# A graph network's edge step on one core: overlapping stages of units, small groups first, and pairs of chunks in one adding scatter

## The chip, the cores and the metric

The kernel runs on one core of one Trainium2 chip. The metric is the time of one execution on the device in microseconds (us). Of the version before there are three runs: 10865.60, 10892.54 and 10880.72 us, median 10880.72 us.

## The reference

12500 nodes have 64 features each; 800000 edges, in random order, name a source and a destination node and have 16 features of their own. Each edge makes a message, messages are summed by destination, and the nodes are updated:

```python
def reference(x, e_attr, src, dst, w_msg, w_upd):
    N, D = x.shape                      # 12500, 64; e_attr is [800000, 16]
    m_in = jnp.concatenate([x[src], x[dst], e_attr], axis=-1)
    msg = _silu(m_in @ w_msg)           # [800000, 64]
    agg = _segment_sum(msg, dst, N)
    return _silu(jnp.concatenate([x, agg], axis=-1) @ w_upd)
```

## The kernel before, in words

**Two pipelines.** The nodes are split into 128 buckets of 98 by destination. First, *binning* writes a record of 17 floats for each edge (its features and one float that codes the source) into the store `st` in DRAM, where each bucket has a stretch of its own. Second, *gathering* takes full tiles of 128 records of one bucket back from the store, gathers the source's part of the product (`A_d`, a row of 64 floats per node, made at the start) and sums the messages into `ACC`. The two run at the same time: one period of the program is one step of binning and one batch of gathering.

**Binning.** A step takes 8 tiles of 128 edges. ACT builds a one-hot of the bucket (`hf`), PE counts (`z`), DVE turns counts into ranks (`rank`) and spreads each record to the slot of its rank (`X`), and PE moves the records to the partition of their bucket by a product with the one-hot (`pl`). Tiles add into `pl` until a *chunk* is full: 8 tiles (at most 24 slots a bucket) for the first N8 = 140 chunks, then 12 tiles (30 slots), so that two chunks end in three steps. At a chunk's end ACT copies `pl` to `blk` (L468), two small DVE operations work out the next places `ptrs` (L481, L482), and POOL writes all 128 rows, 2040 B each, by one indirect DMA (`st<-blk,ptrs`, L486). Slots that no record fills are zeros; the next scatter writes over them.

**Gathering.** A batch is up to 8 tiles. POOL issues one indirect DMA a tile (`g<-A_d,sidx`, L649) into one of four buffers. In later periods the one-hot `q` of destinations in the bucket is made and transposed on PE (`tq`, copied to `qt` by ACT), PE multiplies (`pre`), DVE adds (`g<-pre,g`, L681), ACT applies silu (L682), PE sums over the edges of a tile (`ag`, L698) and DVE adds that to `ACC` (L710). The first gather into a buffer waits for the `ag` matmuls of the batch that used it, four batches before; the other seven gathers do not wait again. A scatter stands between the fourth and the fifth gather of the period after its chunk.

**Groups and stages.** Batches are cut from groups. A group takes whole units of u tiles from the buckets that have them; DVE and PE plan it, and SP then loads its records (`rt<-st`, L569), after waiting for the plan (`rb`, L593). Early, buckets have few full tiles, so the stages in `FIRST` take single tiles, then units of two, with fewer tiles in a group or batch; after them u is 4, with groups of 64 tiles. A stage starts where the one before stopped. When a group may start is fixed while the program is built, by a simulation of random fillings (`Draws`); periods without a batch stand where it could not start. After the last step the rest is gathered in batches without binning, and the nodes are updated.

**Signals.** An engine that waits for another waits for a semaphore that the other raises at the end of an instruction. Each of the `ag` matmuls raises one.

Of the kernel before, what the change touches and what calls it, by code (L numbers as in the profile page):

```python
# [3 lines left out]
F32 = mybir.dt.float32  # L4
# [25 lines left out]
XR = 2 + W  # L30
# [6 lines left out]
FIRST = [(1, 48, BT, (1, 0, 1, 0)), (2, 24, 6, (3, 3, 2, 2))]  # L37
# [7 lines left out]
SUMMED = "the sum that this reads waits for the gathers into its buffer, the older ones there were read ahead of them"  # L45
LISTED = "the work list holds buckets and tiles of the store"


def mpnn_kernel(tc, x, e_attr, src, dst, w_msg, w_upd, out):
# [7 lines left out]
    CAPT = (K8 * S8 + (NCH - K8) * S) // P + 2  # L57
# [3 lines left out]
    NREC = TOP * P  # L61
# [11 lines left out]
    with es:  # L73
# [11 lines left out]
        A_d = dr.tile([NB * BK, D], F32, name="A_d")  # L85
        XU_d = dr.tile([BK, NBK * D], F32, name="XU_d")
        st = dr.tile([NREC, R], F32, name="st")
        st_t = st.rearrange("(t e) c -> t (e c)", e=P)

# [34 lines left out]
        ioS = cb[:, BK:BK + S]  # L124
        hit = cb[:, P:P + M * S].rearrange("p (k s) -> p k s", s=S)
# [3 lines left out]
        nc.vector.tensor_scalar(out=ioS, in0=iof[:, 0:S], scalar1=RK, scalar2=None, op0=OP.add)  # L129

# [7 lines left out]
        ub = {u: cp.tile([NBK, 1], F32, name=f"ub{u}") for u in (1, 2, QU)}  # L138
        nc.vector.tensor_scalar(out=ub[1], in0=ipf, scalar1=float(CAPT), scalar2=None, op0=OP.mult)
        ptr0 = cp.tile([NBK, 1], I32, name="ptr0")  # L140
        nc.vector.tensor_scalar(out=ptr0, in0=ub[1], scalar1=float(P), scalar2=None, op0=OP.mult)
# [3 lines left out]
        capm = cp.tile([NBK, 2 + len(FIRST)], F32, name="capm")  # L145
# [8 lines left out]
        stages = []  # L154
        for i, (u, gt, bt, give) in enumerate(FIRST):
# [7 lines left out]
            stages.append(dict(u=u, gt=gt, bt=bt, cap=cap, caps=caps, total=u * sum(caps)))  # L163
        stages.append(dict(u=QU, gt=GT, bt=BT, cap=None, caps=None, total=None))
# [172 lines left out]
        ACCf = ACC.rearrange("p b k -> p (b k)")  # L337
        for t in X:
            nc.gpsimd.memset(t[:, :, 0:1], 1.0)
        nc.gpsimd.memset(sent, 0.0)  # L340
# [6 lines left out]
        def later():  # L347
# [5 lines left out]
            if len(zeros) == 15:  # L353
                for k in range(P // SR):
                    nc.sync.dma_start(st_t[D0:D0 + DUM, k * SR * R:(k + 1) * SR * R], sent[0:DUM].rearrange("p a b -> p (a b)"))
            elif len(zeros) == 13:
                nc.sync.dma_start(BW[BK:KQ], w_msg[2 * D:2 * D + DE, None, :].to_broadcast([DE, NBK, D]))
# [4 lines left out]
        bp = pool("bp", 2)  # L362
        sm = pool("sm", 4)
        rcp = pool("rcp", 2)
# [6 lines left out]
        state = dict(x=0, rt=0, u=1, ptr=ptr0, done=done0, stage=0, taken=0, straight=True)  # L371

        blocks = []
        gathers = []
# [4 lines left out]
        class Step:  # L379


            def __init__(c, hi, rec, index, n=M):

                c.hi, c.rec, c.n = hi, rec, n
# [4 lines left out]

                c.last = {k: K8 + (index * M + k) // c.size for k in range(n) if c.pos[k] == c.size - 1}  # L390
# [44 lines left out]
            def expand(c, rs=None):  # L435
# [6 lines left out]
                nc.vector.tensor_tensor(out=c.x[:, :, 1], in0=rank, in1=limc[:, c.turn, :], op=OP.is_ge)  # L442
                nc.vector.tensor_tensor(out=hit, in0=ioS[:, None, :].to_broadcast([P, M, S]), in1=rank[:, :, None].to_broadcast([P, M, S]), op=OP.is_equal)
                for k in range(0, c.n, 2):
                    n = LIM[c.pos[k]]
                    nc.vector.tensor_tensor(out=c.x[:, k:k + 2, 2:2 + n * R].rearrange("p k (s c) -> p k s c", c=R), in0=hit[:, k:k + 2, 0:n, None].to_broadcast([P, 2, n, R]),  # L446
                                            in1=c.rec[:, k:k + 2, None, :].to_broadcast([P, 2, n, R]), op=OP.mult)

            def move(c, part=None):
# [4 lines left out]
                for k in reversed(range(c.n)) if whole else range(c.n):  # L454
# [6 lines left out]
                    w = 2 + LIM[n] * R  # L461
                    ends = n == (0 if whole else c.size - 1)
                    nc.tensor.matmul(pl[:, 0:w], c.hf[:, k, :], c.x[:, k, 0:w], start=(n == (c.size - 1 if whole else 0)), stop=ends, skip_group_check=True)  # L463
                    if ends:
                        w = 2 + LIM[c.size - 1] * R
                        end = Chunk(*c.last.values())
                        end.blk = bp.tile([NBK, XR], F32, name="blk")[:, 0:w]
                        nc.scalar.activation(end.blk, pl[:, 0:w], AF.Copy)  # L468
                return end

        class Chunk:


            def __init__(c, index):
                c.index, c.m = index, M if index < K8 else min(C, NT - K8 * M - (index - K8) * C)

            def place(c, ptr_new):

                c.ptr, b = state["ptr"], c.blk
                lost = LOST[:, c.index:c.index + 1]  # L480
                nc.vector.scalar_tensor_tensor(out=lost, in0=b[:, 1:2], scalar=0.0, in1=b[:, 0:1], op0=OP.is_gt, op1=OP.mult)  # L481
                nc.vector.scalar_tensor_tensor(out=ptr_new, in0=b[:, 0:1], scalar=lost, in1=c.ptr, op0=OP.subtract, op1=OP.add)  # L482
                state["ptr"] = ptr_new

            def scatter(c):
                i = nc.gpsimd.indirect_dma_start(out=st, out_offset=bass.IndirectOffsetOnAxis(ap=c.ptr, axis=0), in_=c.blk[:, 2:], in_offset=None)  # L486
                tc.declare_no_dep(i.ins, group="units", reason=WHOLE)
                blocks.append(i.ins)
# [4 lines left out]
        class Group:  # L493


            def __init__(g, u, ptr, done_old, done_new, ceil, gt=GT, base=None, cap=None, bt=BT):
                g.u, g.ptr, g.done_old, g.done_new, g.ceil, g.gt = u, ptr, done_old, done_new, ceil, gt
                g.base = ub[u] if base is None else base
# [688 lines left out]
```

## Time and profile before

| | |
|---|---|
| median of three runs | 10880.72 us |
| profiled execution, own time = its span | 10886.0 us |
| gathers (POOL, L649) | 6322, 949 ns each |
| scatters (POOL, L486) | 567 in the trace, 1000 ns each |
| first gather | at 200.1 us |
| end of binning | near 10083 us |
| mean granted clock of PE | 0.885 |

The span is the time from the first to the last instruction of the profiled execution; the page gives no other time for that execution, so 10886.0 us is what its parts are summed against. A row of costly groups has the line, engine, operation and its names, the count, then busy time and the mean of one in ns, then how long the engine was idle before and what ended that. PEld is PE's load of weights, which overlaps with PE. A share of busy time is a mean over stages that have different limits, so the rows by stretch and the timeline are read beside it.

### The profile page before, as it was taken

What the parts mean: (1) busy time and instruction counts of PE and PEld (TensorE: products, weight loads), DVE (VectorE), ACT (ScalarE), POOL (GpSimd) and SP (SyncE); (2) the same over time, 40 slices, a digit from 0 to 9 for tenths busy, and PEclk for the clock granted to TensorE, in tenths of its full rate; (3) what the DMA queues carried; (4) which work ended last, traced back from release to release, by engine and by line L of the source; (5) the groups of instructions that cost most, each with busy time, mean ns of one, the idle gap of its engine ahead of it and who ended that gap; (6) DMA issues with size and microseconds to landing.
All of it is one profiled execution on the core that took longest, in us unless ns stands there. A gap on an engine that the chain in (4) does not pass through costs nothing. (4 is left out here: it accounts for less than half of the span.)

```text
span 10886.0 us, 155616 instructions
## 1 busy us (share of the span) xinstructions
PE 8949.9 (82%) x49053; PEld 6219.2 (57%) x49816; DVE 7231.4 (66%) x15936; ACT 5082.6 (47%) x12594; POOL 6571.4 (60%) x6908
## 2 busy tenths in 40 slices
PE   8788888888888888888888888888888888888556
PEld 5566655555555555555555555555555555555555
DVE  7777776666666666766666666666666666766232
ACT  6455554444444444444444444444444444544211
POOL 2565666666666666666666666666666666666555
PEclk9999998999989988999998999999899998988555
DMA  3111111111111111111111111111111111111212
GB/s 97 44 49 48 49 49 46 43 47 42 47 42 46 45 44 45 44 43 44 46 43 46 44 44 43 46 47 43 45 42 46 43 47 44 44 45 41 46 36 44
DMA packets 662903, 501.15 MB, mean 46 GB/s; under 512 B 492983, under 2 KB 529911, under 8 KB 662071
## 3 DMA queue, kind: packets, MB, share of 16 engines
q0 software_dynamic: 238976, 349.72, 12.3%
q1 hardware_dynamic: 422775, 141.27, 5.9%
q8 instruction: 400, 6.55, 0.3%
q14 instruction: 432, 3.54, 0.1%
q10 hardware_dynamic: 320, 0.07, 0.0%
HBM read 330.05 MB, written 152.30 MB: 44 GB/s over the span
## 5 line engine op out<-in xcount | busy, mean ns | idle before, releaser
L649 POOL DMA_INDIRECT g<-A_d,sidx x6322 | 5997.6, 949 | 3658.7 <-issue 1620.7
L463 PE MATMUL pl<-X,hf 128*128 128x291 f32 (+5 forms) x12512 | 4745.0, 524 | 476.4 <-issue 428.3
L463 PEld LDWEIGHTS pl<-X,hf 128*128 128x128 f32 x12512 | 2538.7, 211 | 2159.4 <-issue 1737.4
L446 DVE TENSOR_TENSOR X<-cb,rec 128x442 f32<-128x442 f32 (+5 forms) x3128 | 2646.6, 908 | 26.7
L396 ACT ACTIVATE hf<-iof,shi 128x128 f32<-128x128 f32 x6256 | 1908.8, 389 | 1360.4 <-PE pl L463 449.0
L671 ACT ACTIVATE qt<-tq 114x1024 f32<-114x1024 f32 (+1 forms) x818 | 811.7, 992 | 2951.3 <-remote 2298.5
L433 DVE TENSOR_REDUCE rank<-z 128x8 f32<-128x1024 f32 x782 | 954.5, 1221 | 1270.3 <-remote 874.9
L677 PEld LDWEIGHTS pre<-w,qt 114*128 114x128 f32 x10496 | 1392.5, 209 | 687.8 <-ACT qt L671 467.1
L677 PE MATMUL pre<-w,qt 114*128 114x64 f32 x10496 | 1395.2, 291 | 345.6 <-ACT qt L671 317.6
L710 DVE TENSOR_TENSOR ACC<-ag,ACC 64x98 f32 x1938 | 496.7, 256 | 1553.3 <-remote 1131.7
L698 PE MATMUL ag<-q,g 128*64 128x98 f32 x12644 | 882.3, 276 | 490.4 <-remote 236.2
L698 PEld LDWEIGHTS ag<-q,g 128*64 128x64 f32 x12644 | 681.6, 151 | 668.8 <-issue 381.7
L668 PE MATMUL tq<-ident,q 128*114 128x128 f32 x6322 | 929.9, 294 | 103.3 <-issue 91.5
L668 PEld LDWEIGHTS tq<-ident,q 128*114 128x114 f32 x6322 | 812.6, 147 | 238.7 <-issue 122.6
L397 ACT ACTIVATE hf<-hf,ones 128x1024 f32<-128x1024 f32 x782 | 898.8, 1149 | 25.4
L486 POOL DMA_INDIRECT st<-blk,ptrs x567 | 567.2, 1000 | 561.4 <-ACT blk L468 272.2
L659 DVE TENSOR_TENSOR q<-cb,lo 128x784 f32<-128x784 f32 (+1 forms) x818 | 768.7, 940 | 96.1 <-PE ag L698 46.3
L468 ACT ACTIVATE blk<-pl 128x512 f32<-128x512 f32 (+1 forms) x568 | 324.9, 572 | 818.2 <-PE pl L463 500.9
L426 PE MATMUL z<-G,onesb 128*128 128x384 bf16 x1564 | 529.8, 339 | 78.9 <-issue 25.2
L682 ACT ACTIVATE g<-g 128x512 f32<-128x512 f32 (+1 forms) x818 | 498.4, 609 | 192.5 <-DVE g L681 111.8
L681 DVE TENSOR_TENSOR g<-pre,g 128x512 f32<-128x512 f32 (+1 forms) x818 | 541.3, 662 | 51.4 <-issue 37.2
L677 PE MATMUL pre<-BW,qt 114*128 (+1 forms) x2148 | 326.3, 314 | 99.0 <-ACT qt L671 64.8
(138 smaller groups left out, 5243.9 us busy)
## 6 DMA issues: line engine op xcount, KB each, us to landing
g<-A_d,sidx POOLq DMA_INDIRECT x6322
ea<-in_e_attr SPq DMA_DIRECT2D x260, 192.0 KB
rt<-st SPq DMA_DIRECT2D x1312, 34.0 KB
st<-blk,ptrs POOLq DMA_INDIRECT x567
rt<-st SPq DMA_DIRECT2D x434, 8.5 KB
nodes<-in_x SPq DMA_DIRECT2D x62, 98.0 KB
ACC<-rt SPq DMA_DIRECT2D x11, 544.0 KB
rt<-st SPq DMA_DIRECT2D x320, 17.0 KB
```

What stands on the lines that cost most here:

```text
L396: nc.scalar.activation(c.hf[:, k, :], iof, AF.Square, bias=c.hi[:, k:k + 1])
L397: nc.scalar.activation(c.hf, c.hf, AF.Relu, bias=ones, scale=-1.0)
L433: nc.vector.tensor_reduce(out=c.rank, in_=c.z, axis=AX.X, op=OP.max)
L446: nc.vector.tensor_tensor(out=c.x[:, k:k + 2, 2:2 + n * R].rearrange("p k (s c) -> p k s c", c=R), in0=hit[:, k:k + 2, 0:n, None].to_broad ...
L463: nc.tensor.matmul(pl[:, 0:w], c.hf[:, k, :], c.x[:, k, 0:w], start=(n == (c.size - 1 if whole else 0)), stop=ends, skip_group_check=True)
L486: i = nc.gpsimd.indirect_dma_start(out=st, out_offset=bass.IndirectOffsetOnAxis(ap=c.ptr, axis=0), in_=c.blk[:, 2:], in_offset=None)
L649: j = nc.gpsimd.indirect_dma_start(out=t.g[:, i, :], out_offset=None, in_=A_d, in_offset=bass.IndirectOffsetOnAxis(ap=t.grp.sidx[:, k:k + ...
L659: nc.vector.tensor_tensor(out=t.q[:, 0:n, 0:BK], in0=ioB[:, None, :].to_broadcast([P, n, BK]), in1=t.grp.lo[:, i0:i0 + n, None].to_broadca ...
L668: nc.tensor.transpose(t.tq[0:KQ, j * P:(j + 1) * P], t.q[:, j, :], ident)
L671: nc.scalar.activation(t.qt[:, 0:w], t.tq[0:KQ, 0:w], AF.Copy)
L677: nc.tensor.matmul(t.pre[:, i * D:(i + 1) * D], t.qt[:, i * P:(i + 1) * P], w, start=True, stop=True)
L698: o = nc.tensor.matmul(t.ag[t.half(v), v // 2 * BK:(v // 2 + 1) * BK], t.g[:, i, :], t.q[:, i, 0:BK], start=(k == 0), stop=(k == u - 1))
```

## The change

1. **Pairs.** Past chunk 140 two chunks share one scatter. The first is set to the right end of its 30 slots, the second to the left end, so that both are one run of records. ACT copies both to one tile `BLK[128, 2, 510]` and the counts to `cnt`; after the second chunk DVE places the pair by six small operations and POOL issues one indirect DMA that adds (`compute_op=OP.add`, rows of 4080 B). The row begins at the place less the first chunk's empty slots, which overlap records that are there already. A bucket with an overflow in either chunk has its row written aside.
2. **Zeros.** What is added to must be zero: SP writes `st<-Z_d` (271 DMAs from DRAM to DRAM, 522 KB each), LEAD = 4 pieces ahead. A scatter waits for the pieces that it may reach.
3. **One signal for a batch's sums.** Behind the `ag` matmuls stands one more, 8x1, of `ones`; the first gather into the buffer waits for it.
4. **Stages.** 192 single tiles (32 batches of 6) come first instead of 64 (8 batches of 8), then units of two as before. Each stage has a fixed first tile in every bucket, so that stages may overlap: a period tries the stages in order. The groups of the last stage are of 32, 32, 32 and then 64 tiles. Planning has one operation more for each group, and takes account of the slots that a pair's row may reach back.

```diff
-FIRST = [(1, 48, BT, (1, 0, 1, 0)), (2, 24, 6, (3, 3, 2, 2))]
+FIRST = [(1, (12, 12, 24), 6, (2, 1, 2, 1)), (2, (24,), 6, (3, 3, 2, 2))]
+LATER = (32, 32, 32, GT)
...
+        def fill():
+
+            a = (P - S + len(filled) * ROW) * R
+            z = nc.sync.dma_start(st_b[:, a:a + ROW * R], Z_d)
+            tc.declare_no_dep(z.ins, group="blocks", reason=AHEAD)
+            tc.add_to_no_dep_group("zeros", z.ins)
+            filled.append(z.ins)
...
-                        end.blk = bp.tile([NBK, XR], F32, name="blk")[:, 0:w]
-                        nc.scalar.activation(end.blk, pl[:, 0:w], AF.Copy)
+                        end = Chunk(*c.last.values(), c.main)
+                        end.keep(pl, c.right[k])
...
+            def keep(c, pl, right):
+
+                if c.single or c.side == 0:
+                    prior["cnt"] = sm.tile([NBK, 8], F32, name="cnt")
+                c.all = prior["cnt"]
+                c.cnt = c.all[:, 0:4].rearrange("p (a b) -> p a b", b=2)
+                f, a = (0, 2) if right else (W, 0)
+                n = S8 * R if c.single else W
+                if c.main:
+                    nc.scalar.activation(c.cnt[:, c.side, :], pl[:, f:f + 2], AF.Copy)
+                c.blk = BLK[:, c.side, 0:n]
+                nc.scalar.activation(c.blk, pl[:, a:a + n], AF.Copy)
...
             def scatter(c):
-                i = nc.gpsimd.indirect_dma_start(out=st, out_offset=bass.IndirectOffsetOnAxis(ap=c.ptr, axis=0), in_=c.blk[:, 2:], in_offset=None)
+                n = c.index if c.single else K8 + (c.index - K8) // 2
+                at = bass.IndirectOffsetOnAxis(ap=c.ptr, axis=0)
+                if c.single:
+                    i = nc.gpsimd.indirect_dma_start(out=st, out_offset=at, in_=c.blk, in_offset=None)
+                else:
+                    i = nc.gpsimd.indirect_dma_start(out=st, out_offset=at, in_=BLK.rearrange("p a w -> p (a w)"), in_offset=None, compute_op=OP.add)
                 tc.declare_no_dep(i.ins, group="units", reason=WHOLE)
+                tc.declare_no_dep(i.ins, group="zeros", keep=filled[PIECES[n - 1] if n else 0:PIECES[n]], reason=AHEAD)
...
-                            o = nc.tensor.matmul(t.ag[t.half(v), v // 2 * BK:(v // 2 + 1) * BK], t.g[:, i, :], t.q[:, i, 0:BK], start=(k == 0), stop=(k == u - 1))
-                            t.gathers.append(o.ins)
+                            nc.tensor.matmul(t.ag[t.half(v), v // 2 * BK:(v // 2 + 1) * BK], t.g[:, i, :], t.q[:, i, 0:BK], start=(k == 0), stop=(k == u - 1))
+
+                o = nc.tensor.matmul(t.ag[0:t.n, 4 * BK:4 * BK + 1], t.g[:, 0:t.n, 0], ones, start=True, stop=True)
+                t.gathers.append(o.ins)
...
+            if e and not e.whole:
+                e = None
             if e:
                 e.place(ptr_new)
```

POOL in steady state, past chunk 140; `g_220` to `g_223` (before) and `g_243` to `g_246` (after) are the four gather buffers. Before:

```order
L486 DMA st<-blk,ptrs 2938112x17
L649 DMA g_222<-A_d,sidx 128x64 x4
L649 DMA g_223<-A_d,sidx 128x64 x4
L486 DMA st<-blk,ptrs 2938112x17
L649 DMA g_223<-A_d,sidx 128x64 x4
L649 DMA g_220<-A_d,sidx 128x64 x8
```

The same place after:

```order
L739 DMA g_246<-A_d,sidx 128x64 x4
L572 DMA st<-BLK,cnt 2994944x17
L739 DMA g_246<-A_d,sidx 128x64 x4
L739 DMA g_243<-A_d,sidx 128x64 x8
L739 DMA g_244<-A_d,sidx 128x64 x8
L739 DMA g_245<-A_d,sidx 128x64 x4
L572 DMA st<-BLK,cnt 2994944x17
```

Before, two periods in three have a scatter among their gathers; after, one in three.

PE, the middle of a period in steady state. Before:

```order
L428 MATMUL z<-G,onesb 128x512
L668 MATMUL tq<-ident,q 114x128 x8
L698 MATMUL ag<-q,g_222 64x98 x8
L463 MATMUL pl<-X_184,hf 128x461 x2
L463 MATMUL pl<-X_184,hf 128x512 x2
L677 MATMUL pre<-w,qt 128x64 x8
```

After:

```order
L475 MATMUL z<-G,onesb 128x512
L758 MATMUL tq<-ident,q 114x128 x8
L788 MATMUL ag<-q,g_243 64x98 x8
L790 MATMUL ag<-ones,g_243 8x1
L518 MATMUL pl<-X_204,hf 128x461 x2
L518 MATMUL pl<-X_204,hf 128x512 x2
L767 MATMUL pre<-w,qt 128x64 x8
```

The one matmul on `ones` stands between the sums and the moves; the rest of the row is as it was.

SP, between two loads of a group of tiles (`rt`) and the edge features (`ea`, `sdi`, `ssi`). Before:

```order
L569 DMA rt_187<-st 128x68 [waits DMAHW2_49]
L245 DMA ea<-in_e_attr 128x384 [waits DMAHW3_49,Activation_49]
L245 DMA sdi<-in_dst 128x72 [waits DMAHW4_49,DVE_49]
L245 DMA ssi<-in_src 128x72 [waits DMAHW5_49,DVE_49]
L245 DMA ea<-in_e_attr 128x384 [waits DMAHW6_49,Activation_49]
L491 TENSOR_LOAD row [waits DVE_49]
L569 ISA
L569 DMA rt_188<-st 128x68 [waits DMAHW7_49,DMASW1_49]
L569 ISA
```

After:

```order
L415 DMA st<-Z_d 128x1020 [waits DMAHW5_49,DMAHW4_49,DMAHW6_49,DMAHW3_49,DMAHW7_49,DMAHW2_49,DMAHW0_49]
L276 DMA ea<-in_e_attr 128x384 [waits Activation_49]
L415 DMA st<-Z_d 128x1020
L276 DMA sdi<-in_dst 128x72 [waits DVE_49]
L276 DMA ssi<-in_src 128x72 [waits DVE_49]
L579 TENSOR_LOAD row [waits DVE_49]
L659 ISA
L659 DMA rt_206<-st 128x68 [waits DMAHW4_49,DMAHW2_49,DMASW5_49]
L659 ISA
L659 DMA rt_206<-st 128x68
```

The zero writes stand in the queue that also loads edges and groups; the first of them waits for the loads of `rt` before it, and the first load of `rt` behind them for the zero writes.

276 lines of the change are left out of this document (175 added, 101 removed).

## The prediction

> **What bounds the kernel now.** I read the totals first, then busy time by stretch, then the costliest groups, and last POOL's own timeline, since a mean over the span can't tell which wait ends last.
>
> ```profile
> span 10886.0 us, 155616 instructions
> PE 8949.9 (82%) x49053; PEld 6219.2 (57%) x49816; DVE 7231.4 (66%) x15936; ACT 5082.6 (47%) x12594; POOL 6571.4 (60%) x6908
> 0.00:200.00 200.00, 173.88 (x705) 113.08 (x717) 156.37 (x392) 147.39 (x392) 23.33 (x35) 0.97 0.45 116
> 355.00:1531.00 1176.00, 976.23 (x5446) 712.29 (x5549) 896.39 (x2347) 613.56 (x1509) 712.18 (x742) 0.92 0.20 49
> 1531.00:1721.00 190.00, 160.86 (x867) 110.95 (x881) 137.15 (x296) 93.63 (x235) 118.13 (x124) 0.89 0.18 46
> 2700.00:10083.00 7383.00, 6210.02 (x34005) 4216.67 (x34556) 5049.22 (x10659) 3543.55 (x8841) 4581.83 (x4812) 0.91 0.17 44
> 10083.00:10886.00 803.00, 494.93 (x2971) 434.86 (x2969) 211.92 (x551) 148.34 (x293) 453.46 (x481) 0.57 0.23 42
> L649 POOL DMA_INDIRECT g<-A_d,sidx x6322 | 5997.6, 949 | 3658.7 <-issue 1620.7
> L486 POOL DMA_INDIRECT st<-blk,ptrs x567 | 567.2, 1000 | 561.4 <-ACT blk L468 272.2
> ```
>
> The five rows with two times ahead are stretches: length, then the busy time of PE, PEld, DVE, ACT and POOL, the granted clock, the DMA share and GB/s. In the long stretch from 2700 to 10083 PE is busy 6210/7383 = 84%, and yet POOL, at 62%, sets the pace. Its timeline there shows it (start, duration, and in brackets the idle time before):
>
> ```profile
> 5010.81 0.95 POOL L649 DMA_INDIRECT g<-A_d,sidx  x1 [2.44 <-remote]
> 5012.06 0.94 POOL L649 DMA_INDIRECT g<-A_d,sidx  x1 [0.30 <-issue]
> ...
> 5015.81 1.00 POOL L486 DMA_INDIRECT st<-blk,ptrs  x1 [0.31 <-issue]
> 5017.11 0.96 POOL L649 DMA_INDIRECT g<-A_d,sidx  x1 [0.30 <-issue]
> ...
> 5024.34 0.95 POOL L649 DMA_INDIRECT g<-A_d,sidx  x1 [2.52 <-DVE g L681]
> ...
> 5037.83 0.95 POOL L649 DMA_INDIRECT g<-A_d,sidx  x1 [2.48 <-remote]
> ...
> 5049.95 0.95 POOL L649 DMA_INDIRECT g<-A_d,sidx  x1 [2.39 <-remote]
> ```
>
> A gather costs 5012.06 - 5010.81 = 1.25 us, a scatter 5017.11 - 5015.81 = 1.30 us, and after eight gathers POOL stands still for about 2.4 us. A batch with a scatter takes 13.5 us (5010.81 to 5024.34), one without 12.1 us (5037.83 to 5049.95): the pause is the same with and without it, so the scatter's time is on the path. The tail, with no binning beside it and PE at a clock of 0.57, pauses too, so it is not PE's load that makes the pause. What does? The first gather of a batch waits for the eight `ag` matmuls of the batch four before it.
>
> ```profile
> 5016.94 0.38 PE L428 MATMUL z<-G,onesb 128*128 128x512 bf16 x1
> 5017.16 1.04 PE L668 MATMUL tq<-ident,q 128*114 128x128 f32 x8
> 5018.12 0.90 PE L698 MATMUL ag<-q,g 128*64 128x98 f32 x16
> 5022.25 1.22 DVE L433 TENSOR_REDUCE rank<-z 128x8 f32<-128x1024 f32 x1 [1.42 <-remote]
> 5023.77 1.02 ACT L671 ACTIVATE qt<-tq 114x1024 f32<-114x1024 f32 x1 [3.13 <-remote]
> 5024.10 0.53 DVE L710 TENSOR_TENSOR ACC<-ag,ACC 64x98 f32 x2
> 150.65 0.38 PE L428 MATMUL z<-G,onesb 128*128 128x512 bf16 x1
> 151.07 1.23 DVE L433 TENSOR_REDUCE rank<-z 128x8 f32<-128x1024 f32 x1 [0.38 <-PE z L428]
> ```
>
> At 150 us, before any gather, `rank` starts 0.04 us after `z` ends (150.65 + 0.38). At 5017 the records of `z`, `tq` and `ag` end at 5017.32, 5018.20 and 5019.02, and their readers start 4.9, 5.6 and 5.1 us later, `ag`'s 5024.10 just before POOL's 5024.34. While gathers run, PE's completions reach the other engines late; they arrive when POOL has stopped. So POOL waits for signals that come through only once it waits. I read this from times; that the gathers hold the signals back is inferred.
>
> **The sum.** It is made against the profiled execution, 10886.0 us (its span; the page gives no other time), 5 us above the median of 10880.72.
>
> *Scatters.* Past chunk 140 two chunks share one: 568 issues become 140 + 214 = 354, 214 fewer. At 1.30 us that is -278 us; by the batches' difference (13.53 - 12.12 = 1.41) -302. The new ones read 4080 B a partition and add. No row has an adding scatter; bounds are today's 1.00 us of POOL time and twice that (+214 us). I take 1.00, because the gather of 256 B a partition takes 0.95 and this scatter of 2040 B takes 1.00: eight times the bytes cost 0.05.
>
> *Signals.* The eight `ag` matmuls lose their eight signals; one added `ones` matmul behind them signals for all, and the first gather waits for that. It costs 8x1 of work, about the 0.1 us that one `ag` record adds (0.90/16 = 0.06). The nearest rows are two batches of six tiles:
>
> ```profile
> 795.05 0.95 POOL L649 DMA_INDIRECT g<-A_d,sidx  x1 [2.04 <-DVE g L681]
> 805.63 0.94 POOL L649 DMA_INDIRECT g<-A_d,sidx  x1 [1.97 <-PE ag L698]
> 10571.93 0.94 POOL L649 DMA_INDIRECT g<-A_d,sidx  x1 [2.15 <-PE tq L668]
> 10583.84 0.95 POOL L649 DMA_INDIRECT g<-A_d,sidx  x1 [2.20 <-PE tq L668]
> ```
>
> Two tiles, hence two signals, fewer shorten the pause from 2.44 to 2.0 us, 0.22 us a tile, though two tiles less of everything else do part of it. Bounds: +0.1 us a batch (the matmul alone) and -7 x 0.22 = -1.5 us. I take -0.3 on some 690 batches of eight and -0.2 on 136 of six: -234 us. I stay near the first end because most of the pause lies ahead of these signals: `tq`, which keeps its signal, is read only at 5023.77, and `ag` is read 0.33 us behind it; 0.3 is that distance. The other end would need the signals to get through without a pause.
>
> The Trainium skill, on the page TensorE: Matmul & The Clock Gate, section The cost: per-tile semaphore tail, says that increments of a semaphore on every matmul serialize at about 26 ns each and that one on the last is sound. Seven fewer would by it be 0.18 us a batch, an estimate of 150 us over 826 batches, so the sum would be 84 us less of a gain; the delays of about 5 us here are outside that rule, which looks at the tail alone.
>
> *Start.* Before, the first gather comes at 200 us, after 25 steps (8 us each); in the new order after 20, so at 160. Then 136 batches of six at 1176/106 = 11.1 us and one step without a batch (8 us) bring 816 tiles by 1678 us. Before, the same 816 tiles and as many steps are done at 1531 + 14 x 13.3 (190 us for 114 gathers) = 1717. That is -40 us. Later the new order has more steps without a batch and some shorter batches; 546 instead of 514 tiles are left at the last step, so four batches more at 12.0 us (10571.93 to 10583.84 is 11.9), less four steps that cost 8 and not 12.6: +30 us.
>
> *Zeros.* SP issues 271 writes of 522 KB, DRAM to DRAM, four ahead of use.
>
> ```profile
> SPq L491 <- DVE rb L593: 3068.8, 53, 106.6
> GB/s 97 44 49 48 49 49 46 43 47 42 47 42 46 45 44 45 44 43 44 46 43 46 44 44 43 46 47 43 45 42 46 43 47 44 44 45 41 46 36 44
> PE pl L463 <- issue: 428.3, 704, 5.9
> ```
>
> DMA is used to 17% at 44 GB/s, and the fastest slice moved 97 GB/s; at that rate a write lasts 5.4 us, so at worst each shifts the landing of a gather by that, 271 x 5.4 = 1460 us, and at best none does. Only the last gather of a batch, 1.25 us in 12, is waited for at once: I take a tenth, +60 us with the rest rounded in. The same queue stands still for up to 106.6 us in group planning; four pieces ahead are twelve steps, some 145 us, which covers it. Loads of `rt` queue behind a zero write, whose landing they wait for; groups of 64 tiles come every 96 us, so a few us each are hidden. If that cover goes, `sidx` is late and POOL waits.
>
> *Small work.* ACT copies two counters more per chunk and DVE does 4 small operations more per pair, about 0.2 us each: both have room in a batch of 12 us (DVE 68%, ACT 48%). One BLK for all chunks means that ACT's copy waits for the last scatter to land; that was issued two steps ago. Zero. If a landing took over 20 us, `blk` would be late and POOL with it.
>
> Sum: 10886 - 278 - 234 - 40 + 30 + 60 = 10424 us; against the median 10420. In steady batches that is 11.8, 11.8 and 13.1 us: 36.7 for three steps, with PE's 11.2 us a step (84% of 13.3) at 91%. PE stays behind POOL, narrowly.
>
> **Rivals.**
>
> A. *The pause nearly goes.* If one signal gets through between gathers, POOL's pause falls by up to 1.5 us and PE becomes the bound. At 97% busy a step takes 11.5 us, 1.5 us less than 13.0 on 690 batches: with the start and the zeros about 9,900 us. For it: pauses of six tiles are shorter. Against it: `z` and `tq`, with few signals, are as late as `ag`.
>
> B. *No gain from the signals, and PE eats part of the scatters.* 10886 - 278 - 40 + 30 + 60, and a quarter of the scatters' gain lost on PE at 90%: 10,730 us. For it: 84% busy, and 428.3 us of `pl` waiting for nothing that shows. This is also the case in which shared scatters do less than they say.
>
> C. *Slower: the adding scatter is late.* It reads and writes 522 KB in the middle of a batch, and the gathers behind it in the same queue land late. If the pause grows by more than 462/214 = 2.2 us per pair beyond the forecast, all is lost; at 4 us per pair the time is 10424 + 856 = 11,280. For it: POOL's pause already follows the last landing. Against it: five us of gathers follow the scatter and hide that much. The Trainium skill, page DMA: Bandwidth & Descriptors, section Anatomy of one DMA, SWDGE (gpsimd) path, gives 2.0 us plus bytes at 436 GB/s, an estimate of 3.2 us for 522 KB and hidden; no run here has shown an adding one.
>
> D. *No change* within 0.3%, the least that a measurement of this kernel tells from none: B with zeros at 200 us more.
>
> **Numbers.** Forecast (10,300 to 10,550) 0.40; A 0.20; B 0.22; D 0.05; C 0.13. Faster 0.82, same 0.05, slower 0.13. The range leaves out C and all beyond A: 9,900 to 10,850.
>
> **What will show it.** Right: POOL's pause of eight-tile batches near 2.1 us; periods of 11.8 and 13.1; one scatter in three steps at about 1.0 us; first gather near 160 us. A: pauses under 1.2 us and PE over 95%. B: PE's waits small, pauses of 2.4. C: pauses of 4 us and more behind each adding scatter. Wrong altogether if POOL waits on SP's zeros or `sidx`.

## The result: slower, 1.0174 of the time before

The changed kernel takes 11081.49 us (median of four, 11049.0 to 11091.02) against 10886.55 us before: 1.0174 of it, interval 1.0153 to 1.0194. The forecast was 10420 us. The profiled execution spans 11086.9 us, 200.9 more than the one before. Of the runs below, two executions ran in a slower state and count in no ratio, the profiled one of e13 (12683.76 us, at a clock of 0.611) and one of the kernel before beside it (11266.26 us), so e13 has no rows to compare.

POOL sets the pace in both, so its rows are the account. The span and the totals of the engines, from the changed kernel's page:

```profile
span 11086.9 us, 162341 instructions
PE 9032.4 (81%) x50764; PEld 6282.5 (57%) x51528; DVE 7330.5 (66%) x17005; ACT 5101.0 (46%) x13146; POOL 6526.8 (59%) x6696
```

The long stretch in the same columns as before (length, busy PE, PEld, DVE, ACT, POOL, granted clock, DMA share, GB/s): PE is busy 6195/7383 = 84%, as it was.

```profile
2700.00:10083.00 7383.00, 6195.17 (x34484) 4206.33 (x35025) 5012.45 (x11118) 3505.50 (x9084) 4447.52 (x4534) 0.89 0.28 56
```

POOL's three large groups of the changed kernel (busy time, mean ns of one, then the idle time ahead of them and what ended it):

```profile
L739 POOL DMA_INDIRECT g<-A_d,sidx x6322 | 6033.0, 954 | 3572.0 <-issue 1751.7 <-PE ag L790 908.0 <-remote 546.6
L572 POOL DMA_INDIRECT st<-BLK,cnt x214 | 348.1, 1627 | 681.1 <-ACT hf L443 281.9 <-issue 194.5 <-ACT BLK L544 164.8
L570 POOL DMA_INDIRECT st<-BLK,ptrs x139 | 138.9, 999 | 209.4 <-DVE G L452 95.4 <-ACT BLK L544 54.7 <-issue 30.6
```

Busy and idle together, gathers had 5997.6 + 3658.7 = 9656 us before and have 6033.0 + 3572.0 = 9605 now: 51 less. Scatters had 567.2 + 561.4 = 1129 us and have 348.1 + 681.1 + 138.9 + 209.4 = 1378: 249 more, though there are 214 fewer of them in these rows. The two make +198 of the 201 us. So the time is lost at the scatters. Each adding one takes 1.627 us of POOL instead of 1.000, and POOL is idle 681.1/214 = 3.18 us ahead of each.

POOL's timeline of the changed kernel in the steady part, a batch with a pair and the two behind it:

```profile
5029.14 0.95 POOL L739 DMA_INDIRECT g<-A_d,sidx  x1 [0.31 <-issue]
5032.34 0.95 POOL L739 DMA_INDIRECT g<-A_d,sidx  x1 [2.26 <-DMA rt<-st]
...
5036.12 0.94 POOL L739 DMA_INDIRECT g<-A_d,sidx  x1 [0.30 <-issue]
5040.13 1.62 POOL L572 DMA_INDIRECT st<-BLK,cnt  x1 [3.06 <-issue]
5042.05 0.98 POOL L739 DMA_INDIRECT g<-A_d,sidx  x1 [0.30 <-issue]
...
5047.17 0.95 POOL L739 DMA_INDIRECT g<-A_d,sidx  x1 [0.31 <-issue]
...
5059.70 0.94 POOL L739 DMA_INDIRECT g<-A_d,sidx  x1 [2.83 <-remote]
```

After four gathers POOL waits 3.06 us for the pair. The batch that begins at 5047.17 then starts with no pause at all, and the one at 5059.70 with a longer one. A stop has moved from a batch's end to the middle of a batch, and POOL's scatter has grown.

The window is typical: of the 181 pairs between 2700 and 10083 us, 179 are waited for by more than 1 us, and the batch behind a pair starts with a median pause of 0.30 us. From pair to pair, three steps, take 40.6 us in the mean, where two scatters of the kernel before, also three steps, were 39.9 us apart.

Why the pair is not ready shows on the other engines in the same window, in rows of their timelines. PE first:

```profile
5030.97 0.20 PE L790 MATMUL ag<-ones,g 128*8 128x1 f32 x2
5031.10 6.11 PE L518 MATMUL pl<-X,hf 128*128 128x359 f32 x16
```

ACT, which copies the moves out:

```profile
5037.26 0.17 ACT L542 ACTIVATE cnt<-pl 128x2 f32<-128x2 f32 x1 [2.64 <-issue]
5037.32 0.59 ACT L544 ACTIVATE BLK<-pl 128x510 f32<-128x510 f32 x1
```

DVE, with the spreading of the next rows and the first two of the six place operations:

```profile
5035.77 3.01 DVE L500 TENSOR_TENSOR X<-cb,rec 128x442 f32<-128x442 f32 x4
5038.69 0.20 DVE L558 TENSOR_SCALAR cnt<-cnt 128x1 f32<-128x1 f32 x1
5039.11 0.22 DVE L560 SCALAR_TENSOR_TENSOR cnt<-cnt,capm 128x1 int32<-128x1 f32 x1
```

The moves `pl` end at 5037.21, ACT copies to 5037.91, the six place operations queue on DVE behind the spreading that lasts to 5038.78, and the one that the scatter needs ends at 5039.33. The slot behind the fourth gather came at 5037.36. So the copy ends 0.55 us behind the slot, the place another 1.42 us later, and the scatter starts 0.80 us behind that. Counted in the trace over the 181 pairs, the means of the three are 0.97, 1.04 and 0.88 us; with the usual 0.30 ahead of any issue they make up the mean wait of 3.20 us there.

In the kernel before, a scatter has no such place to wait for: its `ptrs` were worked out from the chunk before, and the two operations behind its own copy are for the next scatter. It needs the copy alone, and that ended ahead of the slot, by 1.65 us in the mean of 369 scatters. One of them:

```profile
5027.23 0.60 ACT L468 ACTIVATE blk<-pl 128x512 f32<-128x512 f32 x1 [1.62 <-PE pl L463]
5029.35 1.00 POOL L486 DMA_INDIRECT st<-blk,ptrs  x1 [0.30 <-issue]
```

PE's timeline of the kernel before has the moves of that step here:

```profile
5018.95 1.47 PE L463 MATMUL pl<-X,hf 128*128 128x359 f32 x4
```

They began 5.4 us ahead of the batch at 5024.34; in the changed kernel they begin 1.2 us ahead of theirs (5031.10 against 5032.34). So the batch starts earlier against PE's work. That the one signal does this, in place of eight, is a reading of these rows; e8 and e13 test it, and e13 gives it about half of the loss.

The first gather comes at 189.1 us and not at the forecast 160, by the row of the gathers' line (shortest, median and longest in ns, then the first and last start):

```profile
L739 POOL DMA_INDIRECT g<-A_d,sidx x6322: 939/947/1328, 189.1 to 11044.8; - x198
```

### The profile page after: what moved, and what is told of

Same layout as the page of the kernel before. It is cut to its first block, busy times and chain, and to the rows that moved or that the text cites. A ratio compares the mean times of both kernels' runs of the same rounds, so it can differ in the third digit from the quotient of the medians.

```text
span 11086.9 us, 162341 instructions
## 1 busy us (share of the span) xinstructions
PE 9032.4 (81%) x50764; PEld 6282.5 (57%) x51528; DVE 7330.5 (66%) x17005; ACT 5101.0 (46%) x13146; POOL 6526.8 (59%) x6696
## 5 line engine op out<-in xcount | busy, mean ns | idle before, releaser
L739 POOL DMA_INDIRECT g<-A_d,sidx x6322 | 6033.0, 954 | 3572.0 <-issue 1751.7
L518 PE MATMUL pl<-X,hf 128*128 128x291 f32 (+5 forms) x12512 | 4638.8, 519 | 338.3 <-issue 299.3
L518 PEld LDWEIGHTS pl<-X,hf 128*128 128x128 f32 x12512 | 2492.0, 206 | 1891.5 <-issue 1441.2
L788 PE MATMUL ag<-q,g 128*64 128x98 f32 x12644 | 1003.8, 280 | 702.5 <-issue 521.1
L767 PEld LDWEIGHTS pre<-w,qt 114*128 114x128 f32 x10176 | 1308.6, 202 | 441.4 <-issue 234.5
L767 PE MATMUL pre<-w,qt 114*128 114x64 f32 x10176 | 1291.3, 283 | 132.2 <-ACT qt L761 125.2
L788 PEld LDWEIGHTS ag<-q,g 128*64 128x64 f32 x12644 | 740.8, 153 | 947.5 <-issue 769.0
L572 POOL DMA_INDIRECT st<-BLK,cnt x214 | 348.1, 1627 | 681.1 <-ACT hf L443 281.9
L542 ACT ACTIVATE cnt<-pl 128x2 f32<-128x2 f32 x568 | 96.8, 170 | 1199.0 <-PE pl L518 673.4
L452 DVE TENSOR_TENSOR G<-hf 128x256 bf16<-128x256 f32 x782 | 330.9, 423 | 138.4 <-ACT hf L444 82.8
```

The lines of the kernel that those rows point to most:

```text
L518: nc.tensor.matmul(pl[:, a - o:b - o], c.hf[:, k, :], c.x[:, k, a:b], start=(n == (c.size - 1 if whole else 0)), stop=ends, skip_group_che ...
L739: j = nc.gpsimd.indirect_dma_start(out=t.g[:, i, :], out_offset=None, in_=A_d, in_offset=bass.IndirectOffsetOnAxis(ap=t.grp.sidx[:, k:k + ...
L767: nc.tensor.matmul(t.pre[:, i * D:(i + 1) * D], t.qt[:, i * P:(i + 1) * P], w, start=True, stop=True)
L788: nc.tensor.matmul(t.ag[t.half(v), v // 2 * BK:(v // 2 + 1) * BK], t.g[:, i, :], t.q[:, i, 0:BK], start=(k == 0), stop=(k == u - 1))
```

## The experiments

The chips on which they ran are of two kinds. On two chips the kernel before takes 8910 to 8927 us, on three others, the result's kind, 10735 to 10914 us. Ratios are therefore always against the kernel before on the same chip. The first four runs, e1 to e4, fell on a chip of the faster kind, for which the times that were expected of them, made from the result's chip, say little; e7, e8, e11 and e12 repeat their edits. In brackets are intervals of 95%:

| edit | on chips of 10,735 to 10,914 us | on chips of 8,910 to 8,927 us |
|---|---|---|
| the changed kernel (e5, e15) | 1.0173 [1.0156, 1.0190], 1.0176 [1.0158, 1.0194] | not run |
| changed, scatter last (e7; e1) | 0.989 [0.9873, 0.9906] | 0.997 [0.9958, 0.9981] |
| changed, eight signals (e13; e9) | 1.009 [1.0072, 1.0108] | 0.9958 [0.9944, 0.9972] |
| changed, scatter last and eight signals (e16) | 0.9875 [0.9857, 0.9893] | not run |
| changed, no pairs (e17; e2, e11) | 1.0068 [1.0045, 1.0091] | 1.0046 [1.0029, 1.0063], 1.0049 [1.0032, 1.0065] |
| before, one signal (e8; e3) | 1.0049 [1.0032, 1.0066] | 1.0003 [0.9994, 1.0013] |
| before, scatter last (e14; e10) | 0.9952 [0.9934, 0.9970] | 1.0002 [0.9993, 1.0012] |
| changed, plain pairs with zeros (e6) | 1.0274 [1.0256, 1.0292] | not run |
| changed, plain pairs, no zeros (e4, e12) | not run | 0.9954 [0.9938, 0.9971], 0.9936 [0.9920, 0.9953] |
| changed, scatter last, zeros twice (e18) | 0.9956 [0.9943, 0.9970] | not run |

**The scatter behind all eight gathers (e1, e7).**

```diff
             if q:
-                q.gather(0, BT // 2)
+                q.gather(0, BT)
             if s:
                 s.scatter()
-            if q:
-                q.gather(BT // 2, BT)
```

> The changed kernel with one edit: the scatter of a period stands behind all eight gathers of the batch, not between the fourth and the fifth. Theory P (place): a pair's chunk ends late in its period, so that POOL stops about 3.05 us ahead of 179 of 181 adding scatters in the steady stretch and then again at the batch's end; with the scatter last the two waits fall together: some 200 x 2.5 us less, 10,550 to 10,700 us. Theory T (traffic: zeros and adding writes make every landing late): no change, 11,030 to 11,130. Theory S (signals of PE come through only while POOL stands still, so that a wait saved at one place comes back at the next): the wait ahead of the scatter goes, the batch's wait grows by as much, 10,950 to 11,100.

> The changed kernel with the scatter behind all eight gathers, a second time, for the chip. On a chip of 8,900 us: 0.997 again and no gain on e5, since no scatter waits there. On a chip of 10,880 us: theory P 0.97 to 0.985 of before, theory S 1.005 to 1.02.

On the result's kind of chip 10798.22 us, 0.989 of before: faster than both kernels. On the other kind (e1) 8883.12 us, 0.997. Of the two theories P is right in direction and S wrong there, but P's 0.97 to 0.985 was too good. POOL's groups in e7:

```profile
L739 POOL DMA_INDIRECT g<-A_d,sidx x6322 | 6032.2, 954 | 3893.9 <-issue 1633.9 <-PE ag L790 1619.4 <-remote 326.4
L572 POOL DMA_INDIRECT st<-BLK,cnt x214 | 348.8, 1630 | 97.7 <-issue 57.7 <-ACT BLK L544 17.3 <-DVE LOST L563 13.7
```

And POOL's timeline in e7, the first gather of a batch, the pair's scatter, and the first gathers of the two batches behind it:

```profile
5021.54 0.94 POOL L739 DMA_INDIRECT g<-A_d,sidx  x1 [2.31 <-remote]
5031.59 1.63 POOL L572 DMA_INDIRECT st<-BLK,cnt  x1 [0.30 <-issue]
5035.02 0.98 POOL L739 DMA_INDIRECT g<-A_d,sidx  x1 [1.80 <-PE ag L790]
5047.33 0.94 POOL L739 DMA_INDIRECT g<-A_d,sidx  x1 [2.38 <-PE ag L790]
```

The idle time ahead of pairs fell from 681.1 to 97.7 us, and that ahead of gathers rose from 3572.0 to 3893.9: 583 us taken away, 322 come back. The pause is still there behind the scatter, 1.80 us. A period with a pair takes 13.48 us (5021.54 to 5035.02), one without 12.31.

**No pairs, the rest of the change (e2, e11, e17).** Each chunk past 140 has its own plain scatter of 510 floats; no zeros.

```diff
-                c.right = [not main or c.turn == 2 or c.turn == 3 or (c.turn == 1 and k >= C - M) for k in range(M)]
+                c.right = [True] * M
...
-                c.single = index < K8
+                c.single = True
...
-            while len(zeros) < 16 and len(filled) < min(PIECES[-1], PIECES[min(ahead, len(PIECES) - 1)] + LEAD):
-                fill()
...
```

> The changed kernel without pairs: each chunk past 140 has its own plain scatter again and there are no zeros; the new stages, the fixed first tiles and the one signal per batch stay. Theory P: pairs cost what was lost, the rest gains: 10,550 to 10,750 us. Theory T: the same as P, since zeros and adding go too. Theory S: near the kernel before, 10,800 to 10,900, with shorter waits at the batches' ends and new ones ahead of the scatters.

> The changed kernel without pairs and zeros, with the new stages and the one signal, for the chip of 10,900 us: pairs then account for 1.017 less this. By the one signal alone (1.005) and the stages' -10 us it is 1.000 to 1.008; if the stages bring the -40 us of the prediction and lose nothing later, 0.998. On a chip of 8,900 us 1.0046 again.

> The changed kernel without pairs and zeros. On a chip of 10,900 us: with the one signal's 1.005 and the stages' -10 us, 1.000 to 1.008. On a chip of 8,900 us 1.005 for the third time.

1.0068 on the result's kind and 1.005 on the other: no gain in stages, early groups and one signal together. On the faster kind the one signal alone is at 1.0003 (e3) on the same chip as e2's 1.0046, so what is left there, the stages and the new way of placing and planning, costs 0.4%; by the forecast it gained 10 us. Pairs then account for 1.0174/1.0068, about 1.1% of loss, and with the scatter last for a gain: 0.989/1.0068, about 1.8%. These quotients cross chips of one kind.

**One signal on the kernel before (e3, e8).** The `reduce` of the change put into the kernel before, as in the diff of the change.

> The kernel before with one edit: the eight sums of a batch give one signal, by the matmul on ones behind them. The prediction gave this -234 us: 10,650. Theory S: the wait at the batch's end shortens but comes back elsewhere, 10,830 to 10,900 us. Theories P and T say nothing on it beyond the prediction's 10,650.

> The kernel before with one signal per batch, a second time, for the chip. On a chip of 8,900 us: 1.000 again, since POOL does not wait for the sums there. On a chip of 10,880 us: the prediction's 0.978; theory S 0.995 to 1.002.

1.0049 on the result's kind, where the prediction's term says 0.978 and theory S at most 1.002. POOL's groups there:

```profile
L649 POOL DMA_INDIRECT g<-A_d,sidx x6322 | 6012.4, 951 | 3619.7 <-issue 1637.6 <-remote 1048.7 <-PE ag L700 645.4
L486 POOL DMA_INDIRECT st<-blk,ptrs x567 | 566.6, 999 | 655.9 <-ACT blk L468 376.5 <-issue 157.5 <-ACT nodes L196 99.8
```

Idle time ahead of gathers fell from 3658.7 to 3619.7 (-39), and ahead of scatters it rose from 561.4 to 655.9 (+95), of which `blk` has 104 (272.2 to 376.5). The signals did shorten the batches' pause, by 39 us over 6322/8 = 790 batches, 0.05 us each, and more than that came back at the next thing that POOL waits for. (The rows before are from the result's chip and these from e5's; the changed kernel's rows in the result and in e5 differ by 14 us ahead of the pairs and by less than 1 us ahead of gathers.) In the long stretch the copy now ends 0.84 us ahead of the scatter's slot in the mean, and not 1.65: the batches did begin earlier against the moves.

**Eight signals on the changed kernel (e9, e13).** The same edit undone: each `ag` matmul signals again.

> The changed kernel with the eight signals of the sums back, pairs and zeros and stages as they are. In the runs so far (chip of 10,900 us) the one signal made the kernel before 1.005, with 85 us more ahead of its scatters and 45 us less at the batches' ends. Theory M (moved wait: the one signal lets POOL begin a batch earlier against PE's moves, so that the pair is not ready at its slot): the wait ahead of a pair falls from 3.2 to 1 or 2 us, the batch's pause grows by less, 1.005 to 1.014 of before. Theory P (place alone: the pair ends late whatever the signals): 1.015 to 1.022. On a chip of 8,900 us neither wait is there: 0.995 to 1.000.

> The changed kernel with eight signals, for a chip of 10,900 us. Theory M (the one signal lets POOL begin a batch earlier against PE's moves, so that the pair is not ready): the wait ahead of a pair falls from 3.2 to 1 or 2 us, 1.005 to 1.014 of before. Theory P (place alone): 1.015 to 1.022. On a chip of 8,900 us 0.996 again.

1.009 where the changed kernel on the same chip has 1.0176: theory M's range. About half of the loss hangs on the one signal. That the wait ahead of the pair fell to 1 or 2 us is not shown, since e13 has no rows to compare; the time is. With the scatter last, one signal (0.989) and eight (0.9875) don't differ beyond their intervals, and e16 lies between the two values that were expected:

> The changed kernel with the scatter last and eight signals. On a chip of 10,900 us: by the one signal's 1.005 on the kernel before 0.984; if the one signal helps where no scatter waits, 0.993. On a chip of 8,900 us 0.994 to 0.997.

e16 has the lowest ratio on this kind of chip (10757.22 us), though e7's interval overlaps with its own. Its POOL rows:

```profile
L739 POOL DMA_INDIRECT g<-A_d,sidx x6322 | 6004.7, 950 | 3890.5 <-issue 1623.6 <-PE ag L788 1289.9 <-remote 740.0
L572 POOL DMA_INDIRECT st<-BLK,cnt x214 | 348.7, 1629 | 83.0 <-issue 65.2 <-DVE LOST L563 11.4 <-ACT BLK L544 4.6
```

**The scatter last on the kernel before (e10, e14),** a control.

> The kernel before with its scatters behind all eight gathers: a control for the run with the scatter last, which brought the changed kernel from 1.017 to 0.989. Theory P: of 567 scatters before only some 100 wait, 250 us in all; these go, 0.978 to 0.99 if nothing takes their place. Theory S (PE's completions come through about 2.5 us behind POOL's last issue of any kind): the pause then follows the scatter and is as long; waits ahead of scatters go, the batches' ends take part of it back, 0.985 to 1.000. On a chip of 8,900 us: 0.998 to 1.002.

> The kernel before with the scatter behind all eight gathers, for a chip of 10,900 us. Theory P: the 250 us ahead of some 100 scatters go, 0.978 to 0.99. Theory S (completions come through about 2.5 us behind POOL's last issue of any kind): 0.985 to 1.000. On a chip of 8,900 us 1.000 again.

0.9952 on the result's kind. POOL's groups in e14:

```profile
L649 POOL DMA_INDIRECT g<-A_d,sidx x6322 | 5990.9, 948 | 3817.0 <-issue 1555.7 <-remote 1148.7 <-PE ag L698 805.3
L486 POOL DMA_INDIRECT st<-blk,ptrs x567 | 566.7, 999 | 348.4 <-issue 163.8 <-ACT nodes L196 106.3 <-ACT blk L468 57.9
```

A scatter and the next gather in e14's timeline:

```profile
5021.41 1.00 POOL L486 DMA_INDIRECT st<-blk,ptrs  x1 [0.30 <-issue]
5024.87 0.96 POOL L649 DMA_INDIRECT g<-A_d,sidx  x1 [2.46 <-remote]
```

213 us less ahead of scatters, 158 us more ahead of gathers: three quarters came back, as theory S says. The next gather starts 3.46 us behind the start of the scatter, as it starts some 3.4 us behind the start of the last gather where that is last (0.95 + 2.44). So the pause follows POOL's last issue, whichever it is; in e7 the first gather behind an adding scatter starts 3.43 us behind that scatter's start (5031.59 to 5035.02).

**Plain writes instead of adding (e4, e6, e12).**

```diff
-                    i = nc.gpsimd.indirect_dma_start(out=st, out_offset=at, in_=BLK.rearrange("p a w -> p (a w)"), in_offset=None, compute_op=OP.add)
+                    i = nc.gpsimd.indirect_dma_start(out=st, out_offset=at, in_=BLK.rearrange("p a w -> p (a w)"), in_offset=None)
```

e4 and e12 leave out the calls of `fill()` as well, so that no zeros are written; e6 keeps them.

> The changed kernel with pair scatters that write instead of adding and without the 271 zero writes; a pair's row then writes over part of the records before it, so sums are not computed whole. POOL's and the DMA's work is else the same. Theory T: near the forecast, 10,450 to 10,650 us. Theory P: the wait ahead of the scatter stays, 0.6 us less for each of 214 scatters, 10,900 to 11,000. Theory S: 10,900 to 11,080.

> The changed kernel with pair scatters that write instead of adding; the 271 zero writes stay, and records are lost as in the run without zeros. It splits the two. If zeros' traffic costs: slower than e4 against before (0.995) by the whole difference to e5. If the adding scatter's POOL time costs (1.63 us instead of 1.00): like e4, 0.993 to 0.997 on a chip of 8,900 us; some 214 x 0.63 = 135 us below e5 on a chip of 10,880 us.

> Pair scatters that write, without zeros (records are lost), for the chip of 10,900 us. The run with zeros was 1.027 there. If zeros cost nothing, 1.025 to 1.029; by the prediction's 60 us, 1.021; if zeros' traffic made landings late (each gather ahead of a pair landed at up to 3.9 us), 1.000 to 1.015. On a chip of 8,900 us 0.995 again.

e6 missed: 1.0274, where 135 us less than the changed kernel were expected, and 107 us more were measured. POOL's groups in e6:

```profile
L739 POOL DMA_INDIRECT g<-A_d,sidx x6322 | 6033.1, 954 | 3775.0 <-issue 1782.9 <-PE ag L790 1175.5 <-remote 375.7
L572 POOL DMA_INDIRECT st<-BLK,cnt x214 | 214.0, 1000 | 725.9 <-ACT hf L443 326.7 <-issue 268.1 <-ACT BLK L544 101.2
```

POOL's software queue in e6 (packets, MB, and the time that they took as a share of 16 engines' span):

```profile
q0 software_dynamic: 228704, 349.71, 30.4%
```

The gathers in e5, the changed kernel on the same chip:

```profile
L739 POOL DMA_INDIRECT g<-A_d,sidx x6322 | 6019.5, 952 | 3572.3 <-issue 1800.0 <-PE ag L790 859.6 <-remote 575.4
```

And its software queue:

```profile
q0 software_dynamic: 242400, 349.71, 17.0%
```

A plain pair costs POOL 1.000 us, so the extra 0.63 us belong to the adding. But gathers waited 203 us more, and the same bytes took 30.4% of the DMA engines' time instead of 17.0%. By the landings that the traces hold, a gather landed 3.2 us behind its start in e6 and 2.3 us in e5 (medians), so the transfers were slower as well. The edit changed two things, so neither is priced alone by it; how much of the longer waits comes from the late landings and how much from the shorter stop at the scatter stays open. On the other kind of chip, plain pairs without zeros are at 0.994, and the zeros' own price can't be read from it, since plain pairs with zeros were not run there.

**Zeros twice (e18),** on the kernel with the scatter last.

```diff
+            nc.sync.dma_start(Z2[len(filled) % 4], Z_d)
             z = nc.sync.dma_start(st_b[:, a:a + ROW * R], Z_d)
```

> The changed kernel with the scatter last, and each zero write made twice, the second to a scratch of its own that nobody reads. By the prediction's 60 us for 271 writes: 0.6% above the scatter last, which was 0.989 on a chip of 10,900 us and 0.997 on one of 8,900 us. If zeros hide: the same as those within 0.002. If landings are what POOL waits for, by the up to 2 us that a gather's landing is late behind a zero write: up to 271 x 2 = 540 us, 1.04.

0.9956 against e7's 0.989: 0.66%, some 70 us for 271 more writes. The prediction's term was 60. The two ran on different chips of the result's kind (before 10735 and 10914 us), and the scatter last was not run beside e18, so it is an indication and no price.

**The changed kernel again (e5, e15).**

> The changed kernel as it is, on the chip of these runs. The first four runs fell on a chip on which the kernel before takes 8910 us and POOL never stops between gathers in the steady stretch; there PE's completions are read within about 1 us. Theory C (the chips differ: the late reading of PE's completions, and all of the loss with it, belongs to the chip of the result): where before takes some 8,900 us, this is between the runs with the scatter last (0.997 of before) and the one with plain writes (0.995), 0.993 to 1.000; where before takes some 10,880, it is 1.017 again. Rival (the loss is the change's own, on any chip): 1.010 to 1.020 on both.

> The changed kernel as it is. On a chip of 8,900 us: 0.995 to 0.999 (eight signals gave 0.996, the scatter last 0.997); the rival, a loss of its own on any chip: 1.010 to 1.020. On a chip of 10,900 us 1.017 again.

1.0173 and 1.0176, on two chips of the result's kind: the result comes again. On the other kind it was not run; its variants are at 0.996 (eight signals) and 0.997 (scatter last), so theory C is supported but its own line is open.

## Why the prediction was wrong, step by step

**What bounds the kernel.** Right: POOL, with a pause that follows its last issue. The inference that PE's completions come through only while POOL stands still was in the prediction, and the sum then did not use it: terms were subtracted as if a pause taken away at one place were gone. e14 (158 of 213 us back), e7 (322 of 583) and e8 (95 back for 39) show the opposite. The inference itself can be tested further than the prediction did, because the trace also holds the times at which PE's semaphore was raised. In the prediction's window the two signals of `z` come at 5020.79 and 5022.23, that of `tq` at 5023.74 and the eight of `ag` from 5023.78 to 5024.08, 0.04 us apart, so it is the signals that are late, and not their readers. In the long stretch five of six raises fall into pauses of POOL. That POOL's issuing holds them back is still not shown: on the faster chips POOL issues the same and signals are prompt (last section).

**Scatters, -278 us.** The step that failed first. Taken as 214 x 1.30, at 1.00 us of POOL for an adding one. It costs 1.627, so that 140 x 1.30 + 214 x 1.93 replace 567 x 1.30: -142 us. The reason given, that eight times the bytes cost 0.05 us, did not carry over to an adding write. And the wait ahead of it was held at 0.30 us, as in the timeline; the row of L486, which the prediction shows, has 561.4 us for 567 scatters, 0.99 us each. It became 3.18 us: scatters together +249 us instead of -278, a miss of 527 in a total miss of 661. The prediction let the pair's place work hide on DVE at "zero" because DVE has room in a batch. But it put the place between the copy and the scatter, where none was before, and room in the mean does not help there: of the wait of 3.20 us in the long stretch 0.97 is the copy's lateness, 1.04 the place behind the copy, partly because the spreading stands ahead of it on DVE, and 0.88 the start of the scatter behind the place.

**Signals, -234 us.** Gathers with their idle time came to -51 us in all. On the kernel before the edit alone is +0.5% (e8); on the changed kernel taking it back is -0.8% (e13). The gain of 0.3 us a batch was mis-sized: it is the length of the burst of signals above, but the idle time ahead of gathers fell by 0.05 us a batch in the mean, and the earlier start put the batch ahead of the moves.

The Trainium skill, page TensorE: Matmul & The Clock Gate, section The cost: per-tile semaphore tail, puts the gain of a single increment at about 26 ns for each one left out. The trace doesn't bear out the prediction's estimate of 150 us from it: the idle time ahead of gathers fell by 39 us in e8, and the kernel became slower.

**Start, -40 us, and later +30.** First gather at 189.1 us and not 160: 25 steps became 20, but not at 8 us each. The 816th gather starts at 1716.2 us, and at 1722.7 before, so 6.5 us of the 40 came. The zero writes take a part of it. On one chip, and with the same stages, the first gather comes at 188.5 us with them (e1, first row) and at 174.6 without (e2):

```profile
L739 POOL DMA_INDIRECT g<-A_d,sidx x6322: 938/944/1356, 188.5 to 8861.5; - x198
L739 POOL DMA_INDIRECT g<-A_d,sidx x6322: 938/944/1345, 174.6 to 8926.4; - x198
```

One wait stands out in the changed kernel, ahead of its first scatter, on a zero write:

```profile
L570 POOL DMA_INDIRECT st<-BLK,ptr x1 | 1.1, 1146 | 41.0 <-DMA st<-Z_d 41.0
```

The kernel before has this ahead of its first scatter:

```profile
L486 POOL DMA_INDIRECT st<-blk,ptr x1 | 1.2, 1151 | 31.1 <-ACT nodes L196 31.1
```

The changed kernel's first 160 us, in the columns of the long stretch:

```profile
0.00:160.00 160.00, 123.20 (x492) 80.21 (x501) 103.33 (x269) 106.14 (x298) 15.31 (x29) 0.93 0.63 173
```

DMA is busy 63% at 173 GB/s there, before it was 45% at 116 in 200 us. Of the 41.0 us ahead of the scatter some 10 are new. For all stages together e2 against e3 leaves +0.4% on the faster kind; on the result's kind e17 against e8 leaves +0.2%, across chips and within their intervals.

**Zeros, +60 us.** By e18 of about that size, as an indication alone. The zeros' 14 us ahead of the first gather (e1 against e2) had no term in the prediction.

**The rivals.** C, the slower one, had 0.13 and the right place: POOL stops at the adding scatter, and the price was to decide at 2.2 us a pair. Measured are (249 + 278)/214 = 2.5 us a pair beyond the forecast. Its mechanism was wrong in what it cost: not a late landing behind the scatter, but a pair that is not ready ahead of it. The late landing is there: by the traces an adding pair lands 6.1 us behind its start (median), where the prediction's estimate was 3.2, a scatter before 2.6, and the gather behind it at 4.3 us instead of 2.3. But four gathers follow it, and the next batch starts without a pause. A is refuted on this kind of chip: PE is busy 84% of the long stretch, as before. B was right that the signals bring no gain, and wrong on the scatters.

That the forecast missed is therefore two sizes at the scatter, 1.00 us of POOL for 1.627 and a wait of 0.30 us for 3.18, and a gain of signals that came back elsewhere. One reason why the copy comes so late against POOL is the one signal: with it the copy came 0.8 us later against the slot in the kernel before (e8), and without it about half of the changed kernel's loss goes (e13). What makes the rest of its lateness is open.

## What to carry to other kernels

Where an in-order engine has operations of two pipelines in one row, an operation's cost is its time and whether its data are there when its turn comes; making one pipeline start earlier can turn an operation of the other from free into a stop. Sharing an operation can do the same, where it adds an input: this scatter's place was known a chunk ahead, and the pair's is worked out only behind its second copy. Here putting the scatter at the end of the row was worth 2.8% (1.0173 to 0.989) and cost nothing. And where a pause follows an engine's last issue whatever that is, count what comes back at the next wait before booking a wait as saved.

## What the runs showed of the hardware that was not expected

The same kernel takes 8910 us on some chips and 10,735 to 10,914 on others. On the first, POOL never stops in the steady part; the gathers' group in the kernel before with one signal (e3), which is at 1.0003 of before there:

```profile
L649 POOL DMA_INDIRECT g<-A_d,sidx x6322 | 6014.2, 951 | 1953.7 <-issue 1589.0 <-DMA g<-A_d,sidx 212.4 <-PE z L428 20.3
```

A long stretch of e3, in the same columns:

```profile
2700.00:8100.00 5400.00, 5078.81 (x31319) 3601.88 (x31813) 4541.08 (x9528) 3164.70 (x7919) 4093.17 (x4290) 0.97 0.23 54
```

PE's `tq` in e3's timeline:

```profile
5008.65 1.03 PE L668 MATMUL tq<-ident,q 128*114 128x128 f32 x8
```

And its reader on ACT:

```profile
5010.63 1.00 ACT L671 ACTIVATE qt<-tq 114x1024 f32<-114x1024 f32 x1
```

Idle time ahead of gathers is 1953.7 us, 0.31 each, where the same kernel has 3619.7 on the result's kind (e8); `tq` ends at 5009.68 and is read at 5010.63, 0.95 us later and not 5.6. By the raises of PE's semaphore, the next raise comes 0.01 us (median) behind the end of a matmul that signals, and 2.3 us in e8. PE is busy 94% there, and no edit moved the time by more than 0.7%. So the late completions belong to the chip or to what it ran under, not to the kernel; what holds them back was not found. The granted clock differs too, 0.941 in e3 and 0.886 in e8, and whether that is a cause or comes of PE's waiting is not shown. An adding indirect DMA of 4080 B rows costs POOL 1.627 us to issue and lands 6.1 us behind its start, a plain one 1.000 and 3.2 us, while the plain one keeps the DMA engines busier (30.4% against 17.0%).
